# A replanned transformer block: LayerNorm-2's mean and bias moved to VectorE, and two small DRAM copies ahead of each tile's V loads

## The chip, the cores and the metric

The kernel runs on one NeuronCore of a Trainium2 chip. TensorE (PE) multiplies, VectorE (DVE) and ScalarE (ACT) work on elements, GpSimd (POOL) does a few small operations, and SyncE (SP) issues nearly all DMA transfers in one queue, in order. The 16 DMA engines are shared by all transfers. The metric is the device time of one execution in microseconds (us); lower is better.

## The reference, cut to what matters

One adaLN-conditioned block on 2,048 tokens of width 512, in bf16:

```
sa, ca, ga, sb, cb, gb = (silu(c) @ w_mod).reshape(6, 512)
h = layernorm(x) * (1 + ca) + sa
q, k, v = h @ wqkv                        # 32 heads of 16
# token t attends to tokens t, t-2, ..., t-14 (8 of them), masked below 0
o = softmax(q k^T / 4 + mask) v
x = x + ga * (o @ wo)
h = layernorm(x) * (1 + cb) + sb
x = x + gb * ((silu(h @ w1) * (h @ w3)) @ w2)     # inner width 1792
```

## The kernel before, in words

Tokens are cut into 16 tiles of 128. The code records operations with `p.op` and `p.dma` and does not run them in that order: a fixed list `ORDER` (a permutation of the recorded operations) gives each engine its own in-order list, and `SLOTS` says which buffer or PSUM bank each value takes. `synchronize` adds the semaphore waits that the data need. Numbers such as `C_PQ`, `packet_ns` or the cost arguments of `p.op` and `p.dma` were used to make the list; they are not executed. The list is the result of a planner that knew these costs, and it differs as a whole between the two kernels.

The stages, which overlap:

- **Start.** Warm-up matmuls (`warm`, L496) run on PE while x, the first half of `w_mod`, and `wqkv` are loaded. `modulation(0)` (L475 and L478) makes the scale and shift of LayerNorm 1. `modulation(1)`, the same lines, needs the second half of `w_mod`, which is loaded in two transfers, and makes those of LayerNorm 2.
- **LayerNorm 1** (`ln_stats`): DVE statistics (L533, L534), POOL `rstd` (L538 adds epsilon, L540 raises to -0.5), DVE normalisation (L545). The result is transposed either on PE (L605, with ACT reading PSUM in L613) or by DMA transposes (ACT then works in place, L590). `DMA_T = (3, 2)` says from which group on the DMA does it, for LayerNorm 1 and 2.
- **Projections** (L657 for q and k, L676 for v). V rows go to `v_scratch_dram`, from which each tile's shifted copies for the eight offsets are read back.
- **Attention**, in pairs of tiles: DVE products q·k (`sb_pq`, L707), PE sums over head dimensions (L716), DVE maximum and subtraction (L728, L733), ACT exp (L746), DVE sum, reciprocal, scaling (L758 to L761), PE transposes of the weights (L771). In `values`, four DMA loads of 256 KB each bring a tile's shifted V (`sb_vsh`, `sb_vshx`), each of 128 rows of 2,048 bytes; DVE multiplies (L791), PE sums (L800), ACT evicts (L806), a DMA transposes (`sb_ot`), PE multiplies by `wo` (L824) and DVE adds the residual and sums rows (L828, which gives `sx`).
- **LayerNorm 2** (`ln_sums`), for pairs of tiles: POOL makes the negative mean `nm` (L555); ACT squares with an accumulated sum (L559); POOL makes `rs` (L565, L566) and the bias `nb` (L568); ACT normalises (L570). PE or DMA transposes follow.
- **FFN**: per group of two or four tiles, 14 units of gate and up matmuls (L840), ACT Silu (L846), ACT or DVE evictions and products (L850, L851, L854), then the multiplication by w2 (L883, L871), residual and store (L899).

Each engine works in its own order, so an instruction that waits holds up everything behind it on its engine; the same holds for SP's queue of transfers.

Of the kernel before, what the change touches and what calls it, by code (L numbers as in the profile page):

```python
# [10 lines left out]
P = 128  # L11
S = 2048
D = 512
# [60 lines left out]
class Program:  # L74
# [41 lines left out]
    def dma(self, out, in_, key, packets, r=(), w=(), part=(), after=(), eng="sp", cost=450, group=None, transpose=False,  # L116
            store=False, again=False):
        nc = self.nc

        def fn(e):  # L120
            a = out() if callable(out) else out
            b = in_() if callable(in_) else in_
            with nc.allow_non_contiguous_dma(reason="layout"):
                return e.dma_start(a, b, transpose=True) if transpose else e.dma_start(a, b)  # L124

        n, size = packets
        each = -(-n // 16)
        ns = 600 if transpose else each * (120 if again else packet_ns(size))
        o = self.op(eng, fn, cost, key, r=r, w=w, part=part, after=after, dma=(each, ns, *((900, 200) if store else (1300, 600))))
        if group is not None:  # L130
            group.append(o)
            o.group = group
        return o
# [31 lines left out]
    def synchronize(self):  # L165
# [32 lines left out]
        for o in self.placed:  # L198
            if o.dma:
                first = o.group[0]  # L200
                if first.n not in dsem:
                    dsem[first.n] = self.ctx.enter_context(self.nc.semaphore(f"d{first.n}"))
                o.inc = (dsem[first.n], 16, 16 * len(o.group))
            elif o in waited:
                count[o.eng] += 1
                o.inc = (sems[o.eng], 1, count[o.eng])
# [42 lines left out]
C_PQ, C_RED, C_ACC = 2203, 440, 864  # L249
# [17 lines left out]
NWARM = 14  # L267
NWARM2 = 3
DMA_T = (3, 2)
# [6 lines left out]
def _build(p, A_x, A_wqkv, A_wo, B_w1, B_w3, B_w2, c, w_mod, out):  # L276
# [36 lines left out]
    cst = sb([P, 2], f32, "cst")  # L313
# [28 lines left out]
    v_dram = nc.dram_tensor("v_scratch_dram", (PAD + S, D), bf)  # L342
    PALL = ctx.enter_context(nc.psum_tensor("pall", [P, 8 * 512], f32))
# [40 lines left out]
    p.op("pool", lambda e: e.memset(cst[:, 0:1], EPS), 80, k, part=[vcst])  # L384
    p.op("pool", lambda e: e.memset(cst[:, 1:2], -0.5), 80, k, part=[vcst])
# [30 lines left out]
    p.dma(x_sb[:, 0:2, :], x_view[:, 0:2, :], ("load", 1), (256, 1024), w=vx[0:2])  # L416
# [13 lines left out]
    for dl in range(4):  # L430
        late[f"wo{dl}"] = p.dma(wo[32 * dl:32 * dl + 32, :, :],
              bass.AP(A_wo.tensor, A_wo.offset + dl * D, [[16 * D, H], [4 * D, KT], [1, D]]), ("load", 10), (128, 1024), part=[vwo])
    p.dma(v_dram[0:PAD, :], zrow[:], ("load", 11), (16, 1024), r=[vzrow] + wm_hold, w=[vvpad], store=True)
    for name, a, i in (("wms1", 0, 12), ("wms1b", 512, 26)):
        late[name] = p.dma(wm_s[1][:, :, a:a + 512], wm_view[:, :, 1536 + a:2048 + a], ("load", i), (512, 1024), part=[vwms[1]])
# [55 lines left out]
    def warm(i, after=()):  # L491
# [6 lines left out]
        return p.op("pe", mm, 428 if i < 12 else 218, ("warm", i), r=[vc], w=[vw], after=after)  # L498
# [28 lines left out]
    def ln_stats(Ts):  # L527
# [3 lines left out]
        for T in Ts:  # L531
# [6 lines left out]
        o = p.op("pool", lambda e: e.tensor_tensor(rsn, mv[:, i:i + n, 1], bass.AP(cst, 0, [[2, P], [0, n]]), ALU.add), 320, k,  # L538
                 r=vms + [vcst], w=[va])
        p.op("pool", lambda e: e.tensor_tensor(rsn, rsn, bass.AP(cst, 1, [[2, P], [0, n]]), ALU.pow), 600, k, r=[va, vcst],  # L540
# [10 lines left out]
    def ln_sums(Ts):  # L551
# [3 lines left out]
        p.op("pool", lambda e: e.tensor_scalar(nm[:, i:i + n, 0], sx[:, i:i + n, 0], -1.0 / D, None, op0=ALU.mult), 250, k,  # L555
             r=[vsx[T] for T in Ts], w=[vnm])
        for T, vn in zip(Ts, vns):
            vv = Val("var")
            p.op("act", lambda e, vn=vn, T=T: e.activation(vn.at[:], x_sb[:, T, :], ACT.Square, bias=nm[:, T, :],  # L559
# [5 lines left out]
        o = p.op("pool", lambda e: e.tensor_scalar(rsn, var[:, i:i + n, 0], 1.0 / D, EPS, op0=ALU.mult, op1=ALU.add), 300, k, r=vvs, w=[va])  # L565
        o = p.op("pool", lambda e: e.tensor_tensor(rsn, rsn, bass.AP(cst, 1, [[2, P], [0, n]]), ALU.pow), 600, k, r=[va, vcst],  # L566
                 w=[vr], lead=o)
        p.op("pool", lambda e: e.tensor_tensor(nb[:, i:i + n, 0], nm[:, i:i + n, 0], rsn, ALU.mult), 250, k, r=[vr, vnm], w=[vb], lead=o)  # L568
# [210 lines left out]
    def values(T, i, val):  # L779
# [3 lines left out]
        for q in range(4):  # L783
            p.dma(lambda q=q: vv.at[:, 2 * q:2 * q + 2, :],
                  bass.AP(v_dram, (PAD + T * P + 32 * q) * D, [[2 * D, 16], [-DIL * D, W], [1, 2 * D]]), ("vl", T), (128, 2048),
                  r=[vv_dram[T]] + ([vv_dram[T - 1]] if T else [vvpad]), part=[vv], group=loads, cost=640, again=True)
# [254 lines left out]
```

## Time and profile before

| | us |
|---|---|
| median of 3 runs (245.95 to 248.2) | 246.56 |
| the profiled execution's own time | 248.16 |
| its span, first to last instruction | 246.4 |
| PE busy | 235.0 |
| DVE busy | 166.5 |
| ACT busy | 157.5 |
| POOL busy | 25.7 |

The profile is one execution. Busy time counts a matmul until its modelled end, so that a PE busy for 95% of the span can still be fed too slowly; start-to-start distances tell more. The DMA engines' packets took 62.6% of the span on average on the main queue, nearly all in the first half. Times in the trace are counted from the start of the span.

### The profile page before, as it was taken

To read this page: it belongs to the slowest core of one execution; us is meant where nothing else is said; L and a number is where in the kernel's file an instruction comes from. 1 tells how busy PE (TensorE), PEld (TensorE's weight loads), DVE (VectorE), ACT (ScalarE), POOL (GpSimd) and SP (SyncE) were. 2 spreads that over 40 slices of the span, in tenths; PEclk is the share of its full clock that TensorE was granted. 3 is DMA by queue.
4 is the path that set the end of the run, shared out by engine and by line. 5 is a ranking of instruction groups with operands and counts; after the bars stand their busy time and mean duration, and the time that the engine had idled before them with its cause. 6 is when DMAs were issued, how large, how long until landed. Compare 5 with 4: busy or idle time off the path is not lost.

```text
span 246.4 us, 4593 instructions
## 1 busy us (share of the span) xinstructions
PE 235.0 (95%) x1801; PEld 135.6 (55%) x1801; DVE 166.5 (68%) x271; ACT 157.5 (64%) x329; POOL 25.7 (10%) x71
## 2 busy tenths in 40 slices
PE   7797999999997999999999999999799999999995
PEld 2574554545466785655444444444245555687774
DVE  4699599998985999989999586544402532143362
ACT  2458187999896988678756899735659574142210
POOL 5242110010005000030000003003100010000000
PEclk9999799999999999999999999999999999999999
DMA  6999999999799789696974692582120002010011
GB/s 193 350 309 243 230 204 265 199 256 323 232 249 258 220 229 234 181 236 140 270 169 109 159 262 50 114 201 68 45 64 1 0 9 58 21 45 21 0 45 43
DMA packets 46813, 38.85 MB, mean 158 GB/s; under 512 B 21688, under 2 KB 38088, under 8 KB 46792
## 3 DMA queue, kind: packets, MB, share of 16 engines
q1 hardware_dynamic: 46784, 38.56, 62.6%
q8 instruction: 14, 0.23, 0.4%
q14 instruction: 7, 0.06, 0.1%
q10 hardware_dynamic: 8, 0.00, 0.0%
HBM read 29.62 MB, written 4.21 MB: 137 GB/s over the span
## 4 chain that ended last, share of the span: by engine, by line
PE 63%; DMA 14%; ACT 10%; DVE 5%; SPq 3%; POOL 3%; issue 1%
PE pall L840 34%; PE pall L883 12%; PE pall L824 5%; DMA sb_wqkv<-in_A_wqkv_dram 4%; SPq L124 3%; PE pall L800 3%; PE pall L657 3%; PE pall L871 2%; DMA sb_vsh<-v_scratch_dram 2%; DMA v_scratch_dram<-sb_v 2%; DMA sb_h<-sb_xn 2%; ACT sb_xn L559 2%; ACT sb_h L590 2%; DMA sb_vshx<-v_scratch_dram 2%; PE pall L676 2%; PE pall L716 2%
## 5 line engine op out<-in xcount | busy, mean ns | idle before, releaser
L840 PE MATMUL pall<-sb_h,sb_w 128*128 128x256 bf16 (+1 forms) x672 | 104.4, 308 | 3.6 <-ACT sb_hh L850 1.6
L840 PEld LDWEIGHTS pall<-sb_h,sb_w 128*128 128x128 bf16 x672 | 64.5, 98 | 41.8 <-ACT sb_sg L846 2.7
L846 ACT ACTIVATE sb_sg<-pall 128x256 bf16<-128x256 f32 (+1 forms) x84 | 35.6, 459 | 27.6 <-PE pall L840 21.6
L883 PE MATMUL pall<-sb_w,sb_hh 128*128 128x512 bf16 x196 | 45.2, 379 | 0.0
L707 DVE TENSOR_TENSOR sb_pq<-sb_q,sb_kT 128x4096 bf16<-128x4096 bf16 x16 | 36.4, 2285 | 0.0
L850 ACT ACTIVATE sb_hh<-pall 128x256 bf16<-128x256 f32 (+1 forms) x56 | 25.9, 493 | 13.1 <-PE pall L840 12.9
L791 DVE TENSOR_TENSOR sb_vsh<-sb_vsh,sb_al 128x4096 bf16<-128x4096 bf16 x13 | 29.6, 2288 | 4.5 <-DMA sb_vsh<-v_scratch_dram 3.9
L851 DVE TENSOR_TENSOR sb_hh<-sb_sg,sb_hh 128x256 bf16<-128x256 bf16 (+1 forms) x56 | 17.9, 352 | 21.4 <-ACT sb_hh L850 17.3
L657 PE MATMUL pall<-sb_h,sb_wqkv 128*128 128x512 bf16 (+1 forms) x160 | 32.0, 342 | 0.0
L883 PEld LDWEIGHTS pall<-sb_w,sb_hh 128*128 128x128 bf16 x196 | 19.0, 98 | 20.6 <-issue 0.4
L899 DVE TENSOR_TENSOR sb_o<-pall,sb_x 128x512 bf16<-128x512 f32 (+1 forms) x18 | 11.2, 625 | 16.1 <-PE pall L883 11.7
L657 PEld LDWEIGHTS pall<-sb_h,sb_wqkv 128*128 128x128 bf16 x160 | 14.9, 98 | 12.3 <-issue 0.9
L854 DVE TENSOR_TENSOR sb_hh<-sb_sg,pall 128x256 bf16<-128x256 bf16 x28 | 10.8, 417 | 15.1 <-PE pall L840 11.9
L590 ACT ACTIVATE sb_h<-sb_h,sb_modc 128x512 bf16<-128x512 bf16 (+1 forms) x24 | 16.3, 735 | 4.8 <-DMA sb_h<-sb_xn 4.7
L555 POOL TENSOR_SCALAR sb_nm<-sb_sx 128x2 f32<-128x2 f32 x8 | 3.8, 478 | 133.8 <-DVE sb_x L828 133.8
L676 PE MATMUL pall<-sb_wqkv,sb_h 128*128 128x512 bf16 x64 | 17.3, 395 | 0.3 <-DMA sb_wqkv<-in_A_wqkv_dram 0.3
L824 PE MATMUL pall<-sb_wo,sb_ot 128*128 128x512 bf16 x64 | 15.8, 379 | 0.4 <-DMA sb_ot<-sb_oa 0.4
L828 DVE SCALAR_TENSOR_TENSOR sb_x<-pall,sb_x 128x512 bf16<-128x512 f32 x16 | 10.9, 685 | 7.0 <-PE pall L824 6.9
L570 ACT ACTIVATE sb_xn<-sb_x,sb_nb,sb_rs 128x512 bf16<-128x512 bf16 x16 | 12.7, 820 | 3.8 <-POOL sb_nb L568 3.8
L613 ACT ACTIVATE sb_h<-pall,sb_modc 128x256 bf16<-128x256 bf16 (+1 forms) x18 | 10.2, 624 | 6.9 <-PE pall L605 6.8
L559 ACT ACTIVATE sb_xn<-sb_x,sb_nm 128x512 bf16<-128x512 bf16 x16 | 11.5, 721 | 3.8 <-POOL sb_nm L555 3.7
L666 ACT ACTIVATE sb_kT<-pall 128x512 bf16<-128x512 f32 (+1 forms) x20 | 9.7, 519 | 5.5 <-PE pall L657 5.4
(85 smaller groups left out, 218.8 us busy)
## 6 DMA issues: line engine op xcount, KB each, us to landing
sb_vsh<-v_scratch_dram SPq DMA_DIRECT2D x52, 256.0 KB, 4.8
sb_w<-in_B_w_dram SPq DMA_DIRECT2D x6, 512.0 KB, 7.0
sb_vshx<-v_scratch_dram SPq DMA_DIRECT2D x12, 256.0 KB, 3.9
sb_w<-in_B_w_dram SPq DMA_DIRECT2D x6, 384.0 KB, 5.1
v_scratch_dram<-sb_v SPq DMA_DIRECT2D x16, 128.0 KB, 4.8
out_dram<-sb_o SPq DMA_DIRECT2D x14, 128.0 KB, 1.9
sb_wqkv<-in_A_wqkv_dram SPq DMA_DIRECT2D x3, 512.0 KB, 7.8
sb_x<-in_A_x_dram SPq DMA_DIRECT2D x3, 512.0 KB, 8.2
```

Source lines behind the costliest of these rows:

```text
L559: p.op("act", lambda e, vn=vn, T=T: e.activation(vn.at[:], x_sb[:, T, :], ACT.Square, bias=nm[:, T, :], accum_out=var[:, T, :]), c_act(512 ...
L590: return e.activation(vh.at[:, ft, 0:n * P], vh.at[:, ft, 0:n * P], ACT.Identity, bias=modc[:, 8 * which + ft:8 * which + ft + 1], scale=m ...
L657: ins = e.matmul(bank(vp)[:, 0:n], wqkv[:, t, kind * D + ft * P:kind * D + (ft + 1) * P], vh.at[:, t, 0:n], start=(t == ORDER[0]), stop=(t ...
L676: ins = e.matmul(bank(vp), vh.at[:, t, tt * P:(tt + 1) * P], wqkv[:, t, 2 * D:3 * D], start=(t == ORDER[0]), stop=(t == ORDER[-1]))
L707: return e.tensor_tensor(vp.at[:], in0, in1, ALU.mult)
L791: return e.tensor_tensor(v_w, v_w, a_w, ALU.mult)
L824: ins = e.matmul(bank(vy), vt.at[:, ft, :], wo[:, ft, :], start=(ft == 0), stop=(ft == KT - 1))
L840: ins = e.matmul(bank(vp)[:, 0:n], wt[:, t, fi * P:(fi + 1) * P], vh.at[:, t, 0:n], start=(t == 0), stop=(t == KT - 1))
L846: p.op("act", lambda e: e.activation(vt.at[:, 0:n], bank(vgp)[:, 0:n], ACT.Silu), c_act(n), k, r=[vgp], w=[vt], table="silu")
L850: p.op("act", lambda e: e.activation(vh_.at[:, 0:n], bank(vup)[:, 0:n], ACT.Copy), c_act(n), k, r=[vup], w=[vh_])
L851: p.op("dve", lambda e: e.tensor_tensor(vh_.at[:, 0:n], vt.at[:, 0:n], vh_.at[:, 0:n], ALU.mult), 60 + n * 69 // 128, k, r=[vt], w=[vh_], ...
L883: ins = e.matmul(bank(vz), vhh[fi].at[:, tt * P:(tt + 1) * P], w2[:, fi, :], start=(fi == 0), stop=(fi == NF - 1))
```

## The change

1. **LayerNorm 2.** `nm` and `nb` are made on DVE instead of POOL: `nm` with one multiplication of `sx`, `nb` with one operation from `sx` and `rs`. The factor 1/D moves into the scale of the ACT square, so POOL only adds epsilon and raises to -0.5. LayerNorm 1's epsilon is an immediate now, and the constant that held it is gone.
2. **Skew.** Ahead of the first-recorded of each tile's four V loads stand two copies from DRAM to DRAM, 12 and 4 rows of 8,192 bytes (from `w2` into `skew_dram`, which nobody reads). They add to the same semaphore as the loads, so who waits for a tile's V loads waits for them too. With 16 tiles these are 32 more transfers and 2 MB copied.
3. **Loads.** x is loaded tile by tile for tiles 0 and 1, and tiles 2 and 3 ahead of the first half of `w_mod`; the second half of `w_mod` comes in one transfer instead of two.
4. **Sizes.** 11 + 2 warm-up matmuls instead of 14 + 3; `DMA_T = (4, 2)`, so that LayerNorm 1 of tiles 8 to 11 is transposed on PE instead of by DMA.
5. **The plan.** `ORDER` and `SLOTS` are new as a whole, made with a V packet at 84 ns instead of 120, plus 170 ns for each added copy.

```diff
@@ dma()
+                for pa, pb in pre:
+                    e.dma_start(pa, pb).then_inc(o.inc[0], 16)
                 return e.dma_start(a, b, transpose=True) if transpose else e.dma_start(a, b)
...
-        ns = 600 if transpose else each * (120 if again else packet_ns(size))
+        ns = 600 if transpose else each * ((PACKET if pre == () and not SHIFTED else 84) if again else packet_ns(size)) + 170 * len(pre)
+        o.count = 1 + len(pre)
@@ synchronize()
-                o.inc = (dsem[first.n], 16, 16 * len(o.group))
+                o.inc = (dsem[first.n], 16, 16 * sum(m.count for m in o.group))
@@
-NWARM = 14
-NWARM2 = 3
-DMA_T = (3, 2)
+PACKET = 122
+SHIFTED = True
+NWARM = 11
+NWARM2 = 2
+DMA_T = (4, 2)
@@ loads
-    p.dma(x_sb[:, 0:2, :], x_view[:, 0:2, :], ("load", 1), (256, 1024), w=vx[0:2])
+    for T in range(2):
+        p.dma(x_sb[:, T, :], x_view[:, T, :], ("load", 1), (128, 1024), w=[vx[T]])
-    for name, a, i in (("wms1", 0, 12), ("wms1b", 512, 26)):
-        late[name] = p.dma(wm_s[1][:, :, a:a + 512], wm_view[:, :, 1536 + a:2048 + a], ("load", i), (512, 1024), part=[vwms[1]])
+    late["wms1"] = p.dma(wm_s[1][:], wm_view[:, :, 1536:2560], ("load", 12), (512, 2048), w=[vwms[1]])
@@ ln_sums()
-        p.op("pool", lambda e: e.tensor_scalar(nm[:, i:i + n, 0], sx[:, i:i + n, 0], -1.0 / D, None, op0=ALU.mult), 250, k,
+        p.op("dve", lambda e: e.tensor_scalar(nm[:, i:i + n, 0], sx[:, i:i + n, 0], -D ** -1.5, None, op0=ALU.mult), C_TINY, k,
...
-        p.op("pool", lambda e: e.tensor_tensor(nb[:, i:i + n, 0], nm[:, i:i + n, 0], rsn, ALU.mult), 250, k, r=[vr, vnm], w=[vb], lead=o)
+        p.op("dve", lambda e: e.scalar_tensor_tensor(nb[:, i:i + n, 0], sx[:, i:i + n, 0], -1.0 / D, rsn, op0=ALU.mult, op1=ALU.mult),
+             C_TINY, k, r=[vr] + [vsx[T] for T in Ts], w=[vb])
@@ values()
+            pre = []
+            if SHIFTED and q == 0:
+                for a, b in ((0, 12), (12, 16)):
+                    pre.append((bass.AP(skew, (T * 16 + a) * 4160, [[4160, b - a], [1, 4096]]),
+                                bass.AP(B_w2.tensor, B_w2.offset + (T % 7 * 16 + a) * 8192, [[8192, b - a], [1, 4096]])))
@@ ORDER and SLOTS
...
```

In the new order PE's `modulation(1)` stands behind most of the projections of tiles 0 to 11, at 20.6 us of matmul work after the first V projection, where it stood at 5.5 us before; the first V load stands ahead of all DMA transposes in SP's queue, where four stood ahead of it before. The numbers of instructions for the projections, the attention and the FFN are the same.

More of the change, by code (lines that the diff above doesn't have):

```diff
@@ L116, in dma @@
     def dma(self, out, in_, key, packets, r=(), w=(), part=(), after=(), eng="sp", cost=450, group=None, transpose=False,
-            store=False, again=False):
+            store=False, again=False, pre=()):
         nc = self.nc
@@ L248 @@
 MM = 216
-C_PQ, C_RED, C_ACC = 2203, 440, 864
+C_PQ, C_RED, C_ACC, C_TINY = 2203, 440, 864, 90
 BEFORE = -1e9 / P
@@ L312, in _build @@
     before = sb([P, W, 2, 16], bf, "before")
-    cst = sb([P, 2], f32, "cst")
+    cst = sb([P, 1], f32, "cst")
     st = sb([P, NT, 6], f32, "st")
@@ L342, in _build @@
     v_dram = nc.dram_tensor("v_scratch_dram", (PAD + S, D), bf)
+    skew = nc.dram_tensor("skew_dram", (NT, 16, 4160), bf) if SHIFTED else None
     PALL = ctx.enter_context(nc.psum_tensor("pall", [P, 8 * 512], f32))
@@ L383, in _build @@
     p.op("pool", lambda e: e.memset(mbase[:, 4:8], 1.0), 80, k, part=[vbase])
-    p.op("pool", lambda e: e.memset(cst[:, 0:1], EPS), 80, k, part=[vcst])
-    p.op("pool", lambda e: e.memset(cst[:, 1:2], -0.5), 80, k, part=[vcst])
+    p.op("pool", lambda e: e.memset(cst[:], -0.5), 80, k, w=[vcst])
     k = ("const", 1)
@@ L431, in _build @@
         late[f"wo{dl}"] = p.dma(wo[32 * dl:32 * dl + 32, :, :],
-              bass.AP(A_wo.tensor, A_wo.offset + dl * D, [[16 * D, H], [4 * D, KT], [1, D]]), ("load", 10), (128, 1024), part=[vwo])
+              bass.AP(A_wo.tensor, A_wo.offset + dl * D, [[16 * D, H], [4 * D, KT], [1, D]]), ("load", 10), (256, 1024), part=[vwo])
     p.dma(v_dram[0:PAD, :], zrow[:], ("load", 11), (16, 1024), r=[vzrow] + wm_hold, w=[vvpad], store=True)
-    for name, a, i in (("wms1", 0, 12), ("wms1b", 512, 26)):
-        late[name] = p.dma(wm_s[1][:, :, a:a + 512], wm_view[:, :, 1536 + a:2048 + a], ("load", i), (512, 1024), part=[vwms[1]])
+    late["wms1"] = p.dma(wm_s[1][:], wm_view[:, :, 1536:2560], ("load", 12), (512, 2048), w=[vwms[1]])
     late["wmg1"] = p.dma(wm_g[1][:], wm_view[:, :, 2560:3072], ("load", 13), (512, 1024), w=[vwmg[1]])
@@ L496, in mm @@
             return e.matmul(bank(vw), ones[:, 0:P], ones[:], start=True, stop=True)
-        return p.op("pe", mm, 428 if i < 12 else 218, ("warm", i), r=[vc], w=[vw], after=after)
+        return p.op("pe", mm, 428 if i < 9 else 218, ("warm", i), r=[vc], w=[vw], after=after)
     def gate(i):
@@ L537, in ln_stats @@
         rsn = rs[:, i:i + n, 0]
-        o = p.op("pool", lambda e: e.tensor_tensor(rsn, mv[:, i:i + n, 1], bass.AP(cst, 0, [[2, P], [0, n]]), ALU.add), 320, k,
-                 r=vms + [vcst], w=[va])
-        p.op("pool", lambda e: e.tensor_tensor(rsn, rsn, bass.AP(cst, 1, [[2, P], [0, n]]), ALU.pow), 600, k, r=[va, vcst],
+        o = p.op("pool", lambda e: e.tensor_scalar(rsn, mv[:, i:i + n, 1], EPS, None, op0=ALU.add), 250, k,
+                 r=vms, w=[va])
+        p.op("pool", lambda e: e.tensor_tensor(rsn, rsn, bass.AP(cst, 0, [[1, P], [0, n]]), ALU.pow), 600, k, r=[va, vcst],
              w=[vr], lead=o)
@@ L558, in ln_sums @@
             vv = Val("var")
-            p.op("act", lambda e, vn=vn, T=T: e.activation(vn.at[:], x_sb[:, T, :], ACT.Square, bias=nm[:, T, :],
+            p.op("act", lambda e, vn=vn, T=T: e.activation(vn.at[:], x_sb[:, T, :], ACT.Square, bias=nm[:, T, :], scale=D ** -0.5,
                                                     accum_out=var[:, T, :]), c_act(512) + 212, ("st", NT + T), r=[vx[T], vnm],
@@ L564, in ln_sums @@
         rsn = rs[:, NT + i:NT + i + n, 0]
[L565 to L568, printed above, removed]
+        o = p.op("pool", lambda e: e.tensor_scalar(rsn, var[:, i:i + n, 0], EPS, None, op0=ALU.add), 250, k, r=vvs, w=[va])
+        p.op("pool", lambda e: e.tensor_tensor(rsn, rsn, bass.AP(cst, 0, [[1, P], [0, n]]), ALU.pow), 560, k, r=[va, vcst], w=[vr], lead=o)
+        p.op("dve", lambda e: e.scalar_tensor_tensor(nb[:, i:i + n, 0], sx[:, i:i + n, 0], -1.0 / D, rsn, op0=ALU.mult, op1=ALU.mult),
+             C_TINY, k, r=[vr] + [vsx[T] for T in Ts], w=[vb])
         for T, vn in zip(Ts, vns):
@@ L783, in values @@
         for q in range(4):
+            pre = []
[3 more added lines that the diff above has]
+                                bass.AP(B_w2.tensor, B_w2.offset + (T % 7 * 16 + a) * 8192, [[8192, b - a], [1, 4096]])))
             p.dma(lambda q=q: vv.at[:, 2 * q:2 * q + 2, :],
                   bass.AP(v_dram, (PAD + T * P + 32 * q) * D, [[2 * D, 16], [-DIL * D, W], [1, 2 * D]]), ("vl", T), (128, 2048),
-                  r=[vv_dram[T]] + ([vv_dram[T - 1]] if T else [vvpad]), part=[vv], group=loads, cost=640, again=True)
+                  r=[vv_dram[T]] + ([vv_dram[T - 1]] if T else [vvpad]), part=[vv], group=loads, cost=640 + 450 * len(pre), again=True, pre=tuple(pre))
         def av(e):
```

126 rows, old and new, of tables (ORDER, SLOTS) are left out of this document.

## The prediction

> **What bounds the kernel now.** I read the busy table first, then the granted clock, then PE's idle times in the timeline, then what released them.
>
> ```profile
> PE 235.0 (95%) x1801; PEld 135.6 (55%) x1801; DVE 166.5 (68%) x271; ACT 157.5 (64%) x329; POOL 25.7 (10%) x71
> ...
> PEclk9999799999999999999999999999999999999999
> ```
>
> PE is the bound, and one slice shows a lowered clock. How much of PE's 235 us is work? The chain, read at its end, has these pieces:
>
> ```profile
> 220.73 3.02 PE pall L883 x14
> 223.75 7.86 PE pall L840 x72
> ```
>
> That is 216 ns for 512 columns and 109 ns for 256. Counting all matmuls at such distances (56 ns for a 128-column transpose, 0.44 us for each tile's 16 sums of L716 and 8 of L800) gives: FFN 97.2, w2 48.4, projections 41.5, wo 13.8, L716 and L800 14.0, warm-up 3.7, all transposes and small ones 7.5, together 226.1 us. PE starts at 1.5 and begins its last matmul at 243.5, so it loses 16 us. Taking start-to-start distances less these costs, 4.5 us go before 20 us (loads), 3.3 between 20 and 30, 2.0 between 70 and 80, 2.0 between 170 and 180, and 4.1 in pieces of mostly 0.25 us. The three stretches in the middle are what a new plan can win. PE's timeline around them:
>
> ```profile
> 24.19 0.17 PE L475 MATMUL pall<-sb_mbase,sb_ident 128*128 128x8 bf16 x1 [1.42 <-ACT sb_v L686]
> ...
> 77.40 2.78 PE L840 MATMUL pall<-sb_h,sb_w 128*128 128x256 bf16 x23 [1.57 <-ACT sb_sg L846]
> ...
> 176.59 1.04 PE L840 MATMUL pall<-sb_h,sb_w 128*128 128x512 bf16 x4 [1.65 <-ACT sb_hh L850]
> ```
>
> *The first* is `modulation(1)`. ACT is named, but it had finished at 23.8; the second half of its weights, issued at 12.10 behind all earlier loads, completes in the trace's semaphore events at 24.10 (the view of `sb_wm_s` has 12.0 us as its longest landing), and that is what PE waited for. It costs twice, as the windows show (columns: stretch, then length, PE, PEld, DVE, ACT, POOL busy, clock, DMA share, GB/s):
>
> ```profile
> 22.03:25.45 3.42, 2.00 (x40) 1.18 (x39) 3.42 (x2) 1.79 (x4) 0.00 (x0) 1.00 1.12 257
> 25.45:28.86 3.41, 3.41 (x23) 1.48 (x22) 1.97 (x6) 1.17 (x2) 0.89 (x2) 0.50 1.46 187
> ```
>
> After a stretch with 2.00 us of PE work the clock is halved for 3.41 us: 1.5 us of waiting and 1.7 of slowness. DVE pays too, and DVE has little else to spare (34.0 busy of the 37 us from 29 to 66, where attention feeds the FFN):
>
> ```profile
> 30.18 0.69 DVE L728 TENSOR_REDUCE sb_mx<-pall 128x64 f32<-128x512 f32 x1 [2.76 <-PE pall L716]
> ```
>
> *The other two* are LayerNorm 2 on POOL:
>
> ```profile
> 73.87 2.29 DVE L707 TENSOR_TENSOR sb_pq<-sb_q,sb_kT 128x4096 bf16<-128x4096 bf16 x1
> 74.04 2.19 POOL L555 TENSOR_SCALAR sb_nm<-sb_sx 128x2 f32<-128x2 f32 x1 [18.16 <-DVE sb_x L828]
> ...
> 171.18 2.29 DVE L791 TENSOR_TENSOR sb_vsh<-sb_vsh,sb_al 128x4096 bf16<-128x4096 bf16 x1 [3.10 <-DMA sb_vsh<-v_scratch_dram]
> 171.42 2.11 POOL L568 TENSOR_TENSOR sb_nb<-sb_nm,sb_rs 128x2 f32<-128x2 f32 x1
> ```
>
> A POOL operation that takes 0.2 us elsewhere ends with the long DVE operation that began just before it. ACT's queue waits for it, with Silu evictions behind, and PE runs out of PSUM.
>
> **The change, part by part.**
>
> *`modulation(1)` later, its load in one piece.* It stands 20.6 us of matmul work after the first V projection instead of 5.5, so its weights have some 15 us more. Gone: 1.5 + 1.7 = 3.2 us on PE. Late next is DVE: what PE saves before the FFN counts only if attention comes earlier too. The sums L716 of tiles 0 and 1 need their products, which end at 25.7, so the maximum may start near 27 instead of 30.18: 2.8 of the 3.2 us. Bounds 0 (another wait opens there) and 3.2; I take **-2.8**.
>
> [...]
>
> *`nm` and `nb` on DVE.* Removed: 16 POOL operations, two of which cost PE about 1.7 and 1.8 us. Added: 16 DVE operations of 0.08 to 0.17 us (rows L828's accumulator read and L534), 1.3 to 2.7 us in all, two of them before 66 us. `nm` directly follows L828 on the same engine. But `nb` waits on DVE for POOL's `rs`: two squares at 0.9, L565 at 0.19, L566 at 0.70, and three hops of 0.07 make 2.9 us after `nm`; in the first group the new order puts a reciprocal (0.55), a maximum, a scaling and a subtraction (0.69 each) between, 2.6 us, and the products of tiles 6 and 7 stand behind. I charge 0.5 us there (bounds 0 and 1.5, if ACT comes to the squares late). The two stalls need not both vanish, since POOL still makes `rs` and can meet a long DVE operation twice as before; bounds -3.5 and 0, I take half, **-1.7**, and **+0.5**.
>
> *The skew.* Packets of 2,048 bytes take 84 ns in the first loads of `w_mod`; the 8,192 packets of the V loads average 124 in the trace's records (tenth percentile 84; 142 from 29 to 42 us). If they fell to 84, a tile's 32 packets per DMA engine would save 1.3 us. A row of 8,192 bytes is four such packets, 0.34 to 0.5 us, and an engine with both copies spends up to 1.0. So the loads land between 1 us earlier and 1 us later. They were hardly waited for (DVE 3.9 + 0.5 us in all): **0**, bounds -1 and the rival below.
>
> [...]
>
> *SP's queue.* 32 issues at 0.46 (a `w_mod` load) to 0.59 us (a V load), 15 to 19 us, against four transposes removed at 1.2 to 1.7. Cover: SP waits over 100 us for others. Where it is full, 29.7 to 60.5 us, eight copies add 4 to 5 us, but the transposes that held back the first V load until 29.69 (22.4 to 29.6) are gone or behind it, so it can leave some 5 us earlier: 0.
>
> *The rest.* Four warm-ups fewer (-0.9) and 16 PE transposes more (+0.9) cancel; the first V projection waits for the same megabytes (16.9 us).
>
> *The new order.* The 4.1 us of small waits may grow or shrink; bounds -1 and +7 (as much as the three stretches); I take **+0.5**.
>
> Sum: -2.8 - 1.7 + 0.5 + 0.5 = -3.5 us, a span of 242.9 and 244.7 us for that execution. The execution's own 248.16 lies 1.6 above the median; taken off the median, 246.56 - 3.5 = **243.1 us**.
>
> **Rivals.**
>
> - *All three stretches go and nothing new comes*: -3.2 - 3.5 = -6.7, 239.9 us. For: all are single waits. Against: plans meet others.
> - *The stalls move*: ACT or DVE waits of 1.5 to 2 us appear at LayerNorm 2 as before and the first gain is half kept; -1.4 + 0.5 + 0.5, about 246. For: POOL and DVE still meet, and DVE, in order, now blocks behind `nb`.
> - *Slower: the V loads come late.* The plan counts on 84 ns. If packets stay at 124 and the copies cost 1.0, each tile lands 2.3 us after its planned time, a pair of tiles more. VectorE then waits, in the stretch before 66 us first, PE runs out of projections, and later pairs repeat it: two pairs there at 2 us and four later at 1 us are +8, so 246.56 - 3.5 + 8 = 251. It decides once DVE's waits for V loads pass about 4.4 + 3.5 = 8 us. For: the plan is tight, loads share engines with weights. Against: the first V load leaves earlier.
> - *The skew does nothing*: packets stay at 124 and hide; still 243 to 244.
> - *A cold start*: PE has 2.29 us of work from 4.97 to 8.38 and stays at full clock; the new order has some 1.3 there (two transposes 0.1, two warm-ups 0.4, 24 to 32 small matmuls 0.8). A halved window up to 11.8 would cost about 1.2 us, as PE has no slack from 10.5 to 17: 244.3.
>
> **How the numbers follow.** Forecast with the harmless skew 0.45 and cold start 0.10 (242 to 244.5), all gone 0.09, stalls move 0.20, V loads late 0.16. The range leaves out the best and the worst tenth: 239.8 to 249.8. About 1% (244.1 to 249.0) is what a measurement can tell from no change. Faster: 0.45 × 0.9 + 0.10 × 0.4 + 0.09 = 0.54; slower: 0.16 and a little of the moved stalls, 0.18; same 0.28.
>
> **What would show it.** Right: no halved clock near 25 us, `modulation(1)` without a wait, L728 of tiles 0 and 1 starting before 28, the first L840 near 63 instead of 66 us, no POOL operation over 1 us that ACT waits for, a mean V packet under 100 ns. Wrong: DVE waits for V loads beyond 8 us, DVE idle ahead of `nb`, a halved clock before 12 us, or a wait that no part above names.

## The result

The changed kernel takes **253.62 us** in the median of four executions (252.97 to 254.46) against 247.38 us before (the three executions above and a fourth, 245.95 to 250.52): a ratio of 1.027, 95% interval 1.023 to 1.032. It is slower by 6 us where 243.1 was forecast, and outside the range given, 239.8 to 249.8. Its profiled execution took 254.46 us with a span of 252.5.

The page of the changed kernel, its busy table, granted clock and chain:

```profile
PE 233.6 (93%) x1786; PEld 136.2 (54%) x1813; DVE 168.2 (67%) x287; ACT 157.8 (62%) x329; POOL 23.5 (9%) x54
...
PEclk9799999999999999999999999999999999999999
...
PE 57%; DMA 17%; SPq 11%; DVE 7%; ACT 4%; issue 3%; POOL 0%; ACTq 0%; DVEq 0%
```

The chain before:

```profile
PE 63%; DMA 14%; ACT 10%; DVE 5%; SPq 3%; POOL 3%; issue 1%
```

PE's busy time is that of before (some matmul records are missing), spread over 6 us more. In the chain SP's queue has 11% of the span (28 us) where it had 3% before, and DMA 17% instead of 14%; PE, ACT and POOL gave up shares. Where the chain runs through SP's issues, the work behind started when SP got round to its transfer. L125 is the line that issues the copies (3%); L126 issues all others (8%).

What the engines waited for, in the list of waits (us in total, times, longest):

```profile
ACT sb_v L691 <- DMA v_scratch_dram<-sb_v: 5.3, 3, 3.2
DVE sb_vsh L801 <- DMA sb_vsh<-v_scratch_dram: 4.6, 4, 2.3
PE pall L834 <- DMA sb_ot<-sb_oa: 2.4, 3, 1.4
ACT sb_xn L564 <- DVE sb_nm L560: 2.1, 3, 1.3
PE pall L850 <- DMA sb_w<-in_B_w_dram: 1.6, 1, 1.6
DVE sb_vshx L801 <- DMA sb_vshx<-v_scratch_dram: 1.2, 1, 1.2
```

The same waits before:

```profile
DVE sb_vsh L791 <- DMA sb_vsh<-v_scratch_dram: 3.9, 2, 3.1
ACT sb_v L686 <- DMA v_scratch_dram<-sb_v: 0.4, 1, 0.4
PE pall L824 <- DMA sb_ot<-sb_oa: 0.4, 1, 0.4
```

FFN weights are not in the list of before. ACT's wait for V stores and PE's waits for the transposed attention output and for weights grew from 0.8 us together to 9.3, and all three are for transfers of SP's queue. VectorE's waits for V loads went from 4.4 to 5.8 us only. Summing PE's start-to-start losses of more than 0.6 us after the first 20 us gives 11.6 us against 5.1 before (a little of it missing records; short_copies below, which has them all, loses 9.9).

The first stretch and the one where `modulation(1)` waited before (columns as in the prediction):

```profile
5.44:8.85 3.41, 2.27 (x39) 1.33 (x38) 1.88 (x8) 0.00 (x0) 2.76 (x6) 1.00 0.99 337
8.85:12.27 3.42, 3.18 (x27) 2.52 (x26) 1.83 (x6) 2.46 (x6) 0.00 (x0) 0.50 1.09 369
22.03:25.45 3.42, 3.37 (x44) 2.31 (x43) 2.93 (x4) 3.41 (x7) 0.00 (x0) 1.00 0.96 309
```

The halved clock near 25 us is gone, as forecast, and a halved clock from 8.85 to 12.27 is there, as the rival of the cold start had it. Neither is the same in every execution. Among the profiles of these two kernels and of the experiments below, the new order with this start shows a halved clock before 13 us in nine of fifteen, and the old order shows the one near 25 us in two of three (not in before_copies). VectorE got to the first maxima 1.7 us earlier than before (28.48 instead of 30.18), not 3:

```profile
22.72 4.49 DVE L712 TENSOR_TENSOR sb_pq<-sb_q,sb_kT 128x4096 bf16<-128x4096 bf16 x2 [0.49 <-ACT sb_q L670]
...
28.48 0.66 DVE L733 TENSOR_REDUCE sb_mx<-pall 128x64 f32<-128x512 f32 x1
```

The products stand 1.4 us later than before (22.72 instead of 21.3). From there the gain is lost: the first FFN matmul starts at 68.2 us, before at 65.8 (with the 32 copies ahead of the loads in the new order it lies between 65.2 and 68.8 in six profiles, so this one is among the late ones). The stretch in which it turns, in SP's queue (start, length, instruction, count):

```profile
47.13 0.58 SPq L126 DMA_DIRECT2D v_scratch_dram<-sb_v  x1
47.75 2.50 SPq L126 DMA_DIRECT2D sb_vsh<-v_scratch_dram  x4
50.29 1.52 SPq L125 DMA_DIRECT2D skew_dram<-in_B_w_dram  x2
51.85 0.58 SPq L126 DMA_DIRECT2D sb_vsh<-v_scratch_dram  x1
52.48 1.14 SPq L126 DMA_DIRECT2D sb_w<-in_B_w_dram  x2
53.66 0.50 SPq L126 DMA_DIRECT2D v_scratch_dram<-sb_v  x1
54.20 1.23 SPq L126 DMA_DIRECT2D sb_vsh<-v_scratch_dram  x2
55.47 1.48 SPq L125 DMA_DIRECT2D skew_dram<-in_B_w_dram  x2
56.99 0.58 SPq L126 DMA_DIRECT2D sb_vsh<-v_scratch_dram  x1
57.62 0.58 SPq L126 DMA_DIRECT2D sb_w<-in_B_w_dram  x1
```

SP issues for 11 us with gaps of 0.05 us, 3.0 of the 11 for copies. The first-recorded load of a tile is not always the first that SP issues: here four V loads stand ahead of the first copies, and over all tiles 36 of the 64 V loads leave behind their own tile's copies. The last V load of tiles 2 and 3 leaves at 56.99. Without the copies (the kernel no_copies below) the same stretch is:

```profile
45.45 3.11 SPq L126 DMA_DIRECT2D sb_vsh<-v_scratch_dram  x5
48.60 1.14 SPq L126 DMA_DIRECT2D sb_w<-in_B_w_dram  x2
49.79 0.67 SPq L126 DMA_DIRECT2D v_scratch_dram<-sb_v  x1
50.50 2.05 SPq L126 DMA_DIRECT2D sb_vsh<-v_scratch_dram  x3
```

The chain of the changed kernel in the same stretch shows one of the transfers that stood behind the copies, a V store:

```profile
53.66 7.61 DMA v_scratch_dram<-sb_v
...
61.29 0.61 ACT sb_v L691
```

Executions of the new order without copies differ by up to 6 us from each other, and the ratios leave out those more than 1.5% above the fastest, so the medians of all executions stand beside them.

### The profile page after: what moved, and what is told of

It is laid out like the page before. It is cut to its first block, busy times and chain, and to the rows that moved or that the text cites. A ratio compares the mean times of both kernels' runs of the same rounds, so it can differ in the third digit from the quotient of the medians.

```text
span 252.5 us, 4605 instructions
## 1 busy us (share of the span) xinstructions
PE 233.6 (93%) x1786; PEld 136.2 (54%) x1813; DVE 168.2 (67%) x287; ACT 157.8 (62%) x329; POOL 23.5 (9%) x54
## 4 chain that ended last, share of the span: by engine, by line
PE 57%; DMA 17%; SPq 11%; DVE 7%; ACT 4%; issue 3%; POOL 0%; ACTq 0%; DVEq 0%
PE pall L850 27%; SPq L126 8%; PE pall L893 8%; PE pall L662 7%; DMA sb_ot<-sb_oa 6%; DMA v_scratch_dram<-sb_v 4%; DVE sb_vsh L801 4%; PE pall L834 4%; PE pall L681 3%; SPq L125 3%; DMA sb_w<-in_B_w_dram 2%; PE pall L881 2%; DMA sb_wm_s<-in_w_mod_dram 2%; PE pall L810 2%; PE pall L610 2%
## 5 line engine op out<-in xcount | busy, mean ns | idle before, releaser
L850 PE MATMUL pall<-sb_h,sb_w 128*128 128x256 bf16 (+1 forms) x665 | 101.9, 307 | 2.1 <-DMA sb_w<-in_B_w_dram 1.6
L893 PE MATMUL pall<-sb_w,sb_hh 128*128 128x512 bf16 x187 | 43.0, 379 | 0.6 <-issue 0.3
L662 PE MATMUL pall<-sb_h,sb_wqkv 128*128 128x512 bf16 (+1 forms) x156 | 31.0, 341 | 1.9 <-ACT sb_v L691 1.6
L801 DVE TENSOR_TENSOR sb_vsh<-sb_vsh,sb_al 128x4096 bf16<-128x4096 bf16 x12 | 27.2, 2284 | 5.1 <-DMA sb_vsh<-v_scratch_dram 4.6
L570 POOL TENSOR_SCALAR sb_rs<-sb_var 128x2 f32<-128x2 f32 x8 | 4.1, 510 | 164.5 <-ACT sb_xn L564 164.5
L595 ACT ACTIVATE sb_h<-sb_h,sb_modc 128x512 bf16<-128x512 bf16 (+1 forms) x20 | 13.3, 727 | 8.0 <-DMA sb_h<-sb_xn 8.0
L618 ACT ACTIVATE sb_h<-pall,sb_modc 128x256 bf16<-128x256 bf16 (+1 forms) x22 | 12.9, 658 | 6.8 <-DVE sb_modc L493 6.3
L681 PE MATMUL pall<-sb_wqkv,sb_h 128*128 128x512 bf16 x58 | 14.7, 379 | 0.4 <-issue 0.2
L816 ACT ACTIVATE sb_oa<-pall 128x512 bf16<-128x512 f32 x16 | 9.6, 602 | 7.1 <-PE pall L810 6.5
L691 ACT ACTIVATE sb_v<-pall 128x512 bf16<-128x512 f32 x16 | 9.2, 606 | 6.5 <-DMA v_scratch_dram<-sb_v 5.3
```

What stands on the lines that cost most here:

```text
L595: return e.activation(vh.at[:, ft, 0:n * P], vh.at[:, ft, 0:n * P], ACT.Identity, bias=modc[:, 8 * which + ft:8 * which + ft + 1], scale=m ...
L662: ins = e.matmul(bank(vp)[:, 0:n], wqkv[:, t, kind * D + ft * P:kind * D + (ft + 1) * P], vh.at[:, t, 0:n], start=(t == ORDER[0]), stop=(t ...
L681: ins = e.matmul(bank(vp), vh.at[:, t, tt * P:(tt + 1) * P], wqkv[:, t, 2 * D:3 * D], start=(t == ORDER[0]), stop=(t == ORDER[-1]))
L801: return e.tensor_tensor(v_w, v_w, a_w, ALU.mult)
L850: ins = e.matmul(bank(vp)[:, 0:n], wt[:, t, fi * P:(fi + 1) * P], vh.at[:, t, 0:n], start=(t == 0), stop=(t == KT - 1))
L893: ins = e.matmul(bank(vz), vhh[fi].at[:, tt * P:(tt + 1) * P], w2[:, fi, :], start=(fi == 0), stop=(fi == NF - 1))
```

## The experiments

Against the kernel before, which ran beside each:

| kernel | ratio, 95% interval | median us, (before) |
|---|---|---|
| changed | 1.027, 1.023 to 1.032 | 253.62 (247.38) |
| no_copies | 0.996, 0.992 to 1.001 | 247.35 (246.41) |
| short_copies | 1.024, 1.020 to 1.027 | 252.51 (246.41) |
| before_copies | 1.029, 1.025 to 1.033 | 253.95 (246.41) |
| pool_ln2 | 1.022, 1.019 to 1.026 | 252.35 (246.41) |
| one_copy | 1.005, 1.000 to 1.009 | 248.13 (247.02) |
| own_sem | 1.018, 1.011 to 1.026 | 252.10 (247.02) |
| copies_behind | 0.999, 0.994 to 1.003 | 248.07 (247.02) |
| pool_copies | 1.002, 0.999 to 1.006 | 247.52 (247.02) |
| copies_early | 1.003, 0.998 to 1.008 | 249.35 (246.81) |
| copies_mid | 1.000, 0.997 to 1.004 | 247.08 (246.81) |
| no_copies_pool | 1.011, 1.008 to 1.014 | 249.85 (246.81) |
| no_copies_warm | 0.996, 0.993 to 1.000 | 246.36 (246.81) |
| after_store | 1.026, 1.021 to 1.031 | 253.14 (247.00) |
| no_copies_store | 0.996, 0.992 to 1.000 | 246.51 (247.00) |
| no_copies_store_warm | 0.995, 0.992 to 0.998 | 245.52 (247.00) |
| two_even | 1.020, 1.013 to 1.027 | 253.00 (246.65) |
| copies_late | 1.011, 1.005 to 1.018 | 249.71 (246.65) |
| before_one_copy | 1.008, 1.004 to 1.011 | 248.55 (246.65) |

### The copies or the new order?

The theory from the comparison of the traces: the copies cost, by what they delay. The rival: the new order is slow by itself.

**no_copies**

```diff
-            if SHIFTED and q == 0:
+            if False:
```

> The changed kernel without the 32 copies; order, slots and all the rest as they are. The copies' theory (they delay everything behind them, by their issue of 0.8 + 0.6 us a tile on SP or by their time on the DMA engines): 242 to 246 us, at or below the kernel before, with VectorE's waits for V loads and PE's waits for the transposes of the attention output down to about 2 us together. The plan's theory (the new order has its own late transfers, whatever is copied): 250 to 254, with the V store issued at 53.66 and landing 7 us later still there.

0.996, and the profiled execution 243.39 us, close to what was forecast for the changed kernel. That one is the fastest of ten, whose median is 247.35. Its chain, against 57% for PE above:

```profile
PE 82%; DVE 7%; DMA 6%; SPq 1%; ACT 1%; issue 1%; POOL 0%
```

**before_copies** adds `pre` to `dma()` and the copies to `values()` as the change does, and leaves the old order and all else.

> The kernel before with the 32 copies ahead of the first-recorded load of each tile, in its own order. The copies' theory: slower than the kernel before by 4 us or more, as that order has no room planned for them. The plan's theory: within 2 us of the kernel before (247 to 249), as the copies hide in SP's waits. [...]

1.029. VectorE's waits for `sb_vsh` went from 3.9 to 10.9 us. The same copies cost the same in two orders, one of which never had them: it is the copies. That the rest of the change gains anything is not shown: 0.996 has an interval that includes 1, and by the medians the kernel without copies is 0.9 us slower than the kernel before.

### What of a copy costs: bytes, landing, unequal sizes, or the issue?

**short_copies**

```diff
-[[4160, b - a], [1, 4096]]    (and the same of w2)
+[[4160, b - a], [1, 32]]
```

> The changed kernel with the same 32 copies of 12 and 4 rows, but 64 bytes a row instead of 8,192 (so 12 KB copied in all instead of 2 MB, and the same issues on SP). If the copies cost by their issue on SP (1.4 us a tile, 23 us in all): 252 to 254, like the changed kernel. If they cost by their bytes on the DMA engines (up to 1.0 us a tile and engine): the time of the kernel without copies. [...] If the plan is what costs: 252 to 254 as well, and the kernel without copies too.

1.024: rows of 64 bytes cost nearly what rows of 8,192 do. In the packet records such a row takes 12 ns where the long one takes 398, and an issue on SP lasts 0.73 us where it lasted 0.72. Bytes are out, up to the 0.003 between the two ratios, whose intervals overlap. Nor do the loads land more slowly once they are issued: from the issue of a tile's last V load until its V has landed it takes 4.8 us in the mean of 16 tiles in the changed kernel and 4.7 in short_copies, 5.3 in the kernel before and 5.2 in no_copies. They leave SP later.

**own_sem**: each copy increments a semaphore of its own, which only the end waits for.

```diff
-                    e.dma_start(pa, pb).then_inc(o.inc[0], 16)
+                    e.dma_start(pa, pb).then_inc(self.aside, 16)
-        o.count = 1 + len(pre)
+        o.count = 1
```

> The changed kernel with the copies on a semaphore of their own, which only the end of the program waits for, so that nobody waits for a copy to land with a tile's V. If the completions of the copies hold VectorE up: its waits for V loads fall from 4.6 us to about 1, and the ratio to the kernel before goes to 1.000 to 1.012. If it is the issues on SP, which are unchanged: 1.022 to 1.028.

1.018, between the two ranges that were expected. Nobody waits for a copy to land any more, and most of the loss stays. Whether the rest (0.009, intervals that overlap) is the landing isn't settled.

**copies_behind** issues the two copies after the last of a tile's four loads, on a semaphore of their own as in own_sem.

```diff
-                for pa, pb in pre:
-                    e.dma_start(pa, pb).then_inc(o.inc[0], 16)
-                return e.dma_start(a, b, transpose=True) if transpose else e.dma_start(a, b)
+                ins = e.dma_start(a, b, transpose=True) if transpose else e.dma_start(a, b)
+                if max(o.group, key=lambda m: m.at) is o:
+                    for pa, pb in pre:
+                        e.dma_start(pa, pb).then_inc(self.aside, 16)
+                return ins
```

> The changed kernel with each tile's two copies issued behind its last V load instead of among its loads, on a semaphore of their own: V loads leave SP 1.4 us earlier, everything behind them as late as in the changed kernel. If the late V loads are what costs: near the kernel without copies, a ratio of 0.996 to 1.005. If SP's queue as a whole is what costs (transposes, V stores and weights behind): 1.015 to 1.025.

0.999, against 1.018 for own_sem, which differs only in the place of the copies. As many issues on SP, as many bytes, and the loss is gone: the theory that SP's queue as a whole costs falls too. What costs is standing ahead of V loads. SP's queue in the same stretch as above:

```profile
46.58 3.14 SPq L124 DMA_DIRECT2D sb_vsh<-v_scratch_dram  x5
49.77 1.14 SPq L124 DMA_DIRECT2D sb_w<-in_B_w_dram  x2
50.96 0.51 SPq L124 DMA_DIRECT2D v_scratch_dram<-sb_v  x1
51.51 0.53 SPq L124 DMA_DIRECT2D sb_vsh<-v_scratch_dram  x1
52.08 1.51 SPq L127 DMA_DIRECT2D skew_dram<-in_B_w_dram  x2
53.63 1.22 SPq L124 DMA_DIRECT2D sb_vsh<-v_scratch_dram  x2
54.88 1.47 SPq L127 DMA_DIRECT2D skew_dram<-in_B_w_dram  x2
```

The loads of tiles 2 and 3 are interleaved, so one tile's copies still stand ahead of the other's last two loads: 1.5 us instead of 3.0. From the start of the first V load's issue to the end of the last one's it is 8.3 us; 9.8 in the changed kernel and 7.1 without copies.

**pool_copies**: the same 32 copies, issued by GpSimd behind the power of LayerNorm 2, on a semaphore of their own.

```diff
+        def power(e):
+            ins = e.tensor_tensor(rsn, rsn, bass.AP(cst, 0, [[1, P], [0, n]]), ALU.pow)
+            for T in Ts:
+                for a, b in ((0, 12), (12, 16)):
+                    e.dma_start(...).then_inc(p.aside, 16)
+            return ins
```

> The changed kernel with the same 32 copies issued by GpSimd behind LayerNorm 2's power instead of by SP, on a semaphore of their own: the same number of transfers and bytes, none in SP's queue. SP's theory: a ratio to the kernel before of 0.996 to 1.005, like the kernel without copies. If the transfers themselves cost (their time on the DMA engines, or DRAM): 1.015 or more. A cost of the issues on GpSimd would show as ACT waiting for LayerNorm 2's rs or bias.

1.002. Off SP's queue the same transfers cost nothing that can be measured. They also come later there (from 54 to 203 us, where SP issues them from 25 to 162), so this run alone doesn't tell the queue from the time; copies_behind, which stays in SP's queue, shows that the place ahead of the loads is what matters.

**one_copy**: one copy of 16 rows of 8,192 bytes ahead of each tile's loads.

```diff
-                for a, b in ((0, 12), (12, 16)):
+                for a, b in ((0, 16),):
```

> [...] The theory of SP's issues: about half of the 6 to 7 us come back, a ratio to the kernel before of 1.010 to 1.018 instead of 1.027. The theory of bytes or of transfers in flight: 1.024 or more. [...]

1.005, below both ranges that were expected: more than half of the loss is gone. The same bytes in one issue of 0.65 us. Two things changed at once here, the number of copies and their sizes, so:

**two_even**: two copies of 16 rows of 4,096 bytes.

```diff
-                for a, b in ((0, 12), (12, 16)):
+                for a in (0, 2048):
+                    pre.append((bass.AP(skew, T * 16 * 4160 + a, [[4160, 16], [1, 2048]]), ...
```

> [...] If the number of issues on SP decides (some 1.5 us a tile ahead of the loads): a ratio to the kernel before of 1.020 to 1.028. [...]

1.020, median 253.00, against 1.027 for 12 and 4 rows and 1.005 for one copy: the number of copies ahead of the loads, not their unequal sizes.

**before_one_copy**: one copy of 16 rows in the order of before.

> The kernel before with one copy of 16 rows of 8,192 bytes ahead of each tile's loads, where two of 12 and 4 rows gave a ratio of 1.029. If one issue costs half of two: 1.012 to 1.017. If there is a step between one and two in this order as in the new one: 1.002 to 1.008. If bytes decide: 1.025 or more.

1.008. In both orders one issue costs 0.008 over none, and the two of 12 and 4 rows cost 0.029 to 0.031; by the medians one costs 0.2 and 1.9 us, two cost 5.3 and 7.5. The second is dearer than the first, in an order that was planned with copies and in one that wasn't, so the cost does not go by the time of the issues alone. Why was not settled.

### Which tiles?

**copies_early, copies_mid, copies_late**: the condition gets `and T < 4`, `and 4 <= T < 10`, `and T >= 10`.

> The changed kernel with the copies ahead of the loads of tiles 0 to 3 only (8 of 32). Counting matmul waits above 0.6 us, the changed kernel loses 4.0 us more than the one without copies before 66 us (at 38.2 and 59.1 us) and 3 to 4 later. If a delay in one stretch stays in the end: about half of the cost, a ratio to the kernel before of 1.010 to 1.018, with the first matmul of the FFN near 67 instead of 63. If later slack takes it back: 0.996 to 1.005.

> The changed kernel with the copies ahead of the loads of tiles 4 to 9 only (12 of 32), the stretch from 66 to 113 us in which SP was issuing for 48 of 54 us. If SP's fullness decides: the larger part of the cost, a ratio of 1.015 to 1.022. If every tile counts alike: 12 of 32 of 6.5 us, 1.006 to 1.014. If only tiles 0 to 3 count: 0.996 to 1.004.

> The changed kernel with the copies ahead of the loads of tiles 10 to 15 only (12 of 32). If the late tiles carry what tiles 0 to 3 and 4 to 9 did not show: 1.012 to 1.020. If the cost is that of a delay which adds up over all tiles and which the slack takes back when it is only a part: 0.996 to 1.006.

Over the 0.996 without copies these are 0.007, 0.004 and 0.015, together 0.026 of the 0.031 of all; by the medians 1.6, -0.7 and 2.1 us of 5.3. The first two came out where a delay that later slack takes back was expected, the third just below the range in which the late tiles carry the cost. By the ratios the parts add up within their intervals, which are wide; the medians add up to 3.0 us only, so part of the cost may come from the copies of several stretches together. Tiles 10 to 15, which I had not had in view, carry the largest part by both, 0.4 to 0.5 of the whole: V loads are issued until 171 us, well behind the first half of the span. That SP is fullest from 66 to 120 us (48.3 of 54 us issuing, before 37.2) is true and is not where it costs most: copies_mid is the smallest of the three, though its interval overlaps that of copies_early. SP's share of time in use does not tell where a delay matters.

### One late store

In the changed kernel ACT waits 3.2 us at 58 us, and PE behind it, for the V store of tile 5, which was ready at 47.5 and stood behind V loads and weights. Two executions of nearly the same order without copies show the same instruction, first no_copies (243.39 us), then no_copies_warm (its profiled execution took 248.05):

```profile
56.17 0.60 ACT L691 ACTIVATE sb_v<-pall 128x512 bf16<-128x512 f32 x1 [0.57 <-DMA v_scratch_dram<-sb_v]
```

```profile
59.33 0.60 ACT L693 ACTIVATE sb_v<-pall 128x512 bf16<-128x512 f32 x1 [3.75 <-DMA v_scratch_dram<-sb_v]
```

The store was issued at 49.8 and 49.9 and landed 6.4 and 9.4 us later. That looked like the place of both the cost and the spread. **after_store, no_copies_store** and **no_copies_store_warm** move one entry of `ORDER`, the store 233, ahead of the first of those loads, 418:

```diff
-    ... 418, 410, ... 420, ... 408, ... 417, 41, ... 48, ... 233, ...
+    ... 233, 418, 410, ... 420, ... 408, ... 417, 41, ... 48, ...
```

> The changed kernel, copies and all, with one entry of the order moved: the V store of tile 5 stands ahead of the V loads of tiles 2 and 3 in SP's queue. If the store's place carries the cost of the copies: the 2.6 us wait at 59 us goes and the ratio to the kernel before falls from 1.027 to 1.008 to 1.016. If the cost is spread over V loads, transposes and weights: 1.018 to 1.026, with the wait gone but made up for by later ones.

> The changed kernel without copies and with the V store of tile 5 ahead of the V loads of tiles 2 and 3. If that store's wait is what spreads the executions between 243.4 and 249.6 us: a spread below 3 us, a ratio to the kernel before of 0.983 to 0.990 (243 us), no wait of ACT on a V store above 1 us. If DMA engines slow down everything alike: ratio near 0.996 and a spread as wide as without the move.

1.026 and 0.996: the wait went (tile 5's store lands 2 us after its issue), and the time did not change. In after_store ACT then waits 1.9 us at 62.8 us for the next V store; the executions of no_copies_store still spread from 244.6 to 249.5 us, where less than 3 us was expected. The V loads of tiles 2 and 3, behind which it had stood, landed at 60.7 and 62.6 us in no_copies_store, at 60.2 and 62.3 in no_copies_warm (57.1 and 59.2 in no_copies). The most visible wait was a symptom; the theory falls.

### LayerNorm 2 and the start

**pool_ln2** and **no_copies_pool** put `nm` and `nb` back on POOL, with the scales of before, in the same places of the order.

```diff
-        p.op("dve", lambda e: e.tensor_scalar(nm[:, i:i + n, 0], sx[:, i:i + n, 0], -D ** -1.5, ...
+        p.op("pool", lambda e: e.tensor_scalar(nm[:, i:i + n, 0], sx[:, i:i + n, 0], -1.0 / D, ...
-        p.op("dve", lambda e: e.scalar_tensor_tensor(nb[:, i:i + n, 0], sx[:, i:i + n, 0], -1.0 / D, rsn, ...
+        p.op("pool", lambda e: e.tensor_tensor(nb[:, i:i + n, 0], nm[:, i:i + n, 0], rsn, ALU.mult), ...
```

> The changed kernel with the mean and bias of LayerNorm 2 back on GpSimd (with the scales of before), in the same places of the order. My step (the move to VectorE saves 1.2 us): 254 to 256. The rival (VectorE in order makes them wait for V loads and long products, so the move costs): 251 to 253. If neither matters: within 0.7 us of 253.6.

> The changed kernel without the copies and with LayerNorm 2's mean and bias back on GpSimd in the same places. My step (VectorE saves 1.2 us here): a ratio to the kernel before of 1.000 to 1.009, 1.2 us over the kernel without copies, with ACT waiting some 5 us for GpSimd's nm and nb. If it makes no difference: 0.994 to 1.001.

With copies 1.022 against 1.027: the time fell into the rival's range of 251 to 253 us, but the intervals overlap, so no difference is shown. Without them 1.011 against 0.996, medians 249.85 and 247.35: the move to VectorE is worth 2 to 4 us there, more than the 1.2 that I booked. The waits of no_copies_pool name it:

```profile
ACT sb_xn L574 <- POOL sb_nb L572: 5.1, 3, 2.8
ACT sb_xn L564 <- POOL sb_nm L560: 3.0, 2, 1.6
```

In no_copies, where VectorE makes both, ACT waits 1.8 us for `nb` and 1.9 for `nm`. The order was made for VectorE, so this is what the move is worth within this order.

**no_copies_warm**: two warm-up operations of three matmuls, one of them ahead of the first transposes.

```diff
-            return e.matmul(bank(vw), ones[:, 0:P], ones[:], start=True, stop=True)
+            for _ in range({7: 3, 8: 3}.get(i, 1)):
+                ins = e.matmul(bank(vw), ones[:, 0:P], ones[:], start=True, stop=True)
+            return ins
```

> The changed kernel without the copies and with more warm-up work from 5.0 to 8.3 us: two of the warm-up operations do three matmuls instead of one, and one of them stands ahead of the first transposes. If the lowered clock at 8 to 12 us costs what I reckoned (0.5 to 1.2 us): a ratio to the kernel before of 0.987 to 0.995 and no lowered clock before 20 us. If the start is bound by VectorE's normalisation and the loads anyway: within 0.3 us of the kernel without copies, near 0.996. If more work delays modulation: slower by up to 0.6 us.

> As the last, and with the added warm-up work from 5.0 to 8.3 us. If the lowered clock at 8 to 12 us costs 0.5 to 1.2 us: a ratio 0.002 to 0.005 below that of the last, with no lowered clock before 240 us. If the start is bound elsewhere: the same ratio within 0.002.

No lowered clock before 59 us in the one profile, and none before 240 in the other; but six of the fifteen profiles without the added work have none before 40 us either, so these two do not show that the work keeps the clock up. The ratios are 0.996 and 0.995 against 0.996 and 0.996 without the added work, and the medians are each 1 us lower, within the spread. What the cold start costs is not settled: the ratios put it at nearly nothing, but each has an interval of about 1 us either way, which leaves room for the 1.2 us of the prediction. No_copies_store_warm, at 0.995 (0.992 to 0.998), is faster than both kernels, though by half a per cent.

## Why the prediction was wrong, step by step

- **SP's queue: 0.** This is the step that failed. The working had the issues about right (15 to 19 us; it was 23) and covered them with "SP waits over 100 us for others". A sum of waits over the whole span is no cover for an issue that stands directly ahead of a load. The experiments put 0.025 to 0.031 here (the changed kernel less pool_copies, copies_behind and no_copies, and before_copies less the kernel before), 5 to 8 us: two issues of 0.72 us ahead of V loads, in 16 tiles. Part of the cover was right: the first V load does leave earlier, at 22.2 us instead of 29.7. By tiles 2 and 3 little of that is left; their last load leaves at 56.99 us, before at 56.65.
- **The skew: 0, bounds -1 to the rival.** The term was right for the bytes. No run shows which rows one DMA engine takes, so the 1.0 us for an engine with both copies was an estimate alone; a row of 8,192 bytes took 0.398 us on average, within the 0.34 to 0.5 reckoned. The copies came with a mean packet of about 120 ns against 124 before, not under 100. The median fell from 106 to 84 ns, in the changed kernel, with 64-byte rows and with one copy of 16 rows alike. So neither the split into 12 and 4 rows nor the bytes are needed for that, and it bought no time.
- **The rival of late V loads, 251 at 0.16,** came nearest (253.6), in part by luck. It had the V loads late and the packets near 124 ns, but it priced those packets and the copies' time on the engines, which short_copies rules out, and wanted VectorE to wait over 8 us for V. VectorE waited 5.8; the delay showed as waits of ACT for V stores and of PE for the transposed attention output and for weights, which no part named.
- ***modulation(1)* later: -2.8.** The wait and the halved clock went, as forecast, though before_copies, which has the old order, has no halved clock there either; so the 1.7 us reckoned for it are not paid in every execution. The first maximum (L728, now L733) started at 28.48, and at 27.5 to 28.8 in four profiles without copies, instead of near 27; in the changed kernel the products before it begin 1.4 us later. The first FFN matmul was forecast near 63 us: it is at 63.1 in no_copies' fastest execution, 64.4 to 67.3 in others of this order without copies, and 65.2 to 68.8 with all of them ahead of the loads.
- **LayerNorm 2: -1.7 + 0.5.** Right in sign without copies, and too small there (-2 to -4). With copies nothing of it can be seen. ACT's waits for `nm` and `nb` fell from 7.5 to 4.1 us. One POOL operation over 1 us is left: `rs` (L570) took 2.12 us at 79.21, beside a VectorE operation of 2.29 us from 78.96, as POOL's `nm` and `nb` did before; the working had named that and booked half of the gain for it. ACT did not wait for it here: its normalisation at 83.24 follows other work without a gap, so the sign (no such operation that ACT waits for) held in this profile.
- **The new order: +0.5, bounds -1 to +7.** Without copies the whole change measures 0.996, some -1 us (-2 to +0.2), and +0.9 by the medians, where the sum said -3.5 with nothing for SP. At least 2.5 us are missing, then, and the waits for V stores and for the transposed attention output, which come and go between executions (ACT waits 4.2 us for V stores in no_copies_warm, 0.8 in no_copies), would belong here. But that is a subtraction: no run separates this term from the others, and what makes the transfers slower in one execution than in another is open.
- **The cold start** came (8.85 to 12.27) in this profile, and in others of the same start it didn't. That little work of PE in a stretch halves the clock in the next was an estimate from few stretches of one profile (2.00 us from 22.03, halved behind it; 2.29 us from 4.97, not), and it failed: the stretch ahead of it held 2.27 us of PE's work, not the 1.3 that was reckoned, as much as the 2.29 us after which the clock stayed full in the kernel before. So PE's work in a stretch does not by itself tell what the clock does next. Whether it cost the 1.2 us is not settled.

Fewer transfers were better in these runs: one copy of 128 KB costs 0.008, two of 64 KB 0.024, two of 96 and 32 KB 0.031, and rows of 64 bytes almost as much as long ones. That the size decides, they do not show. The prediction put no price on two transfers instead of one; the rows of SP's issues held the time to start from.

## What to carry to other kernels

An added transfer holds back whatever stands behind it in the same queue for the time of its issue, 0.6 to 0.8 us here whatever its size. What that costs ran from nothing to 0.031 of the time here, so look at what is directly behind it and who waits for that, not at how long the queue idles in all. If it must be there, put it behind the urgent loads (0.999 here) or on another engine's queue (1.002), and make it one transfer instead of two (1.005 against 1.027). And test the most visible wait by removing it before believing that it is the cost.

## What the runs showed of the hardware

- An issue on SP did not get shorter with the bytes of a row: 12 and 4 rows of 8,192 bytes took 0.72 us on average (0.81 and 0.62), of 64 bytes 0.73, 16 rows 0.60 to 0.65, a V load of 128 rows of 2,048 bytes 0.59 in the median.
- A packet of 8,192 bytes, nearly all of them the DRAM-to-DRAM rows of the copies, took 398 ns in the changed kernel's records (median 384), 4.7 times the 84 ns of a quick V packet of a quarter of its size.
- The same V store, issued at the same time behind the same transfers, landed 6.4 us after its issue in one execution (no_copies) and 9.4 in another (no_copies_warm).
- After nearly the same work of PE in the 3.41 us before, 2.29 us (before, 4.97 to 8.38) and 2.27 us (changed, 5.44 to 8.85), the clock stayed full in one and was halved in the other.
